# Inverse spectra of a long convolution: tiles of 128 rows, or slots of 32 rows

## The chip, the core and the metric

The kernel runs on one core of one Trainium2 chip. That core has five engines with queues of their own: PE (matrix products into PSUM), DVE (vector), ACT (activation and copies), POOL (general purpose) and SP (issues DMAs). The profile shows PE's weight loads as a sixth row, PEld. The metric is the device time of one execution in microseconds, lower being better. The kernel before has a median of 608.51 us in 3 runs (606.69 to 613.0).

## The reference

`u` has 2048 positions (L) and 640 channels (D). Two branches are mixed by a gate computed from the input.

```
dt = exp(log_dt);  A = -exp(log_A_real) + 1j * A_imag;  C = (C_real + 1j * C_imag) * dt
P  = exp((A * dt)[:, :, None] * pos)                       # 640 x 128 x 2048
K  = 2.0 * einsum("dn,dnl->dl", C, P).real                 # the filter of each channel
a  = irfft(rfft(u_t, 4096) * rfft(K, 4096), 4096)[:, :, :2048] + u * D_skip
b  = irfft2(rfft2(x) * (w_r + 1j * w_i))                   # over positions and channels
g  = sigmoid((x * gate_w).sum(-1));   out = g * a + (1 - g) * b
```

The change is in branch `a`, in the product of the two spectra and the transform back.

## The kernel before, in words

All transforms are matrix products in fp32. The 640 channels are worked in four column chunks `c` of 160. A transform of length 4096 is split in two stages. Stage one (`stage1`) turns blocks of the input into 33 partial spectra, one for each residue `k` of 0 to 32 (the others follow by symmetry), and ACT copies them into the tile `t1`. Stage two (`stage2`) multiplies the slice of one `k` by a 128x128 table (`w2`), as two matmuls with 64 output columns each: real and imaginary part of 64 frequencies. Two residues share the 128 PSUM lanes; such a pair is called a group here, and there are 16 groups and a half one (`k` = 32).

The program has these parts. `phase_a` computes the spectra of `u` and stores them in DRAM (`u_d`), then computes branch `b`, whose last tiles go to DRAM as `s3e_d`. `phase_b` computes the filters `K` beside it and stores them in `k_d`. `phase_c` begins with the filters' stage one for chunk 0. `phase_d` does the rest, and all edits that change instructions lie in it:

- `fronts` computes stage two of the filter for two groups at a time into one two-bank PSUM tile (`p_s`), and multiplies it by the spectrum of `u` (`us`, loaded from `u_d` on ACT's queue): `ma` (L798) holds the products re x re and im x im, `mb` (L799) the crossed ones. The difference (L803) and the sum (L804) go to `t2`, real parts on lanes 0 to 63 and imaginary on 64 to 127, each for one `k`. Since each output of 64 lanes comes from one half of `ma` or `mb`, there are four such instructions of 64 lanes for two groups, two on DVE and two on POOL.
- `backs` multiplies `t2` by the inverse table `w3`, one 128x128 table per `k`, as two matmuls of 64 columns (`p_i`, L817), ACT copies the PSUM tile to `s3`, and a DMA on ACT's queue stores it in `s3_d`.
- `load_c` loads `s3_d` again with the lanes exchanged (`t`, issued by SP), and `last_c` does the last inverse stage (`p_c`, L896), multiplies by the gate into `ot` and adds branch `b`. `load_e` and `last_e` do the like for branch `b` (`t3e` from `s3e_d`, `p_e`, L161, then `oe`, L879).
- `first` is the filter's stage one for the next chunk (`p_s`, L336).

A chunk has five steps: four of four groups and one of the half group. In each step `merge` interleaves three streams by due times: `mains` (fronts of this step, then backs of a step two earlier: `late` holds two), `last_e` or `last_c`, and `first`. The order on each engine is then settled by a scheduler that follows this program order and its own estimates of when operands are ready. Each engine works strictly in its own order.

PSUM has eight banks: in `phase_d` a pool `c_ps` of three tiles of two banks, shared by stage one, stage two and the inverse step, and a pool `d_ps` of two banks for `p_e` and `p_c`. A tile is taken in turn; its next user waits until the reader of the last one is done.

Of the kernel before, what the change touches and what calls it, by code (L numbers as in the profile page):

```python
# [49 lines left out]


def _tables():
# [14 lines left out]
    e3 = np.zeros((64, 2, 2, 32))  # L67
    for j in range(2):
        e3[:, j, j, :] = kr

    e3e = np.zeros((32, 4, 4, 32))
    for r in range(4):
# [3 lines left out]
        e1[0], e1[1], e3.reshape(4, 32, 64).swapaxes(0, 1).reshape(128, 64), e3e.reshape(128, 128), np.eye(128), one,  # L76
# [7 lines left out]
    c, s = np.cos(ph), np.sin(ph)  # L84
    w2 = np.concatenate([np.concatenate([c, -s], 2), np.concatenate([s, c], 2)], 1)
# [7 lines left out]
    w3 = np.swapaxes(w3, 0, 1).reshape(128, NP * 128)  # L93
# [37 lines left out]
    return {"t_c1": f(c1), "t_w2": f(w2), "t_w3": f(w3), "t_td": f(td),  # L131
# [3 lines left out]
def _lay_out(u, log_a, a_i, c_r, c_i, log_dt, d_skip, w_r, w_i, gate_w):  # L135

    ul = u.reshape(32, 64, 4, 40, 4).transpose(2, 4, 0, 3, 1)[:, JR][..., A_ORDER].reshape(4, 128, 40, 64)
    f = (np.arange(18).reshape(9, 2, 1) + 32 * np.arange(64)) % L
# [46 lines left out]
def body(tc, A, out):  # L185
    nc = tc.nc
    T = Ctx()
    with ExitStack() as top:
# [3 lines left out]
        T.s3_d = dram.tile([4, 64, 64, 160], F32, name="s3_d")  # L192
# [161 lines left out]
def phase_a(tc, A, T):  # L354
# [90 lines left out]
    with ExitStack() as ctx:  # L445
# [25 lines left out]
        def front(pr, st):  # L471
            nl = st.nl = 128 if pr < 8 else 64
            st.w3 = w3p.tile([128, 2, 128], F32, tag="w3", name="w3")
            nc.sync.dma_start(st.w3[:, 0:nl // 64, :], w3v[:, 16 + 2 * pr:16 + 2 * pr + nl // 64, :])
# [262 lines left out]
def phase_c(tc, A, T, ctx):  # L737
# [10 lines left out]
    T.w3 = T.cc.tile([128, NP, 128], F32, name="w3")  # L748
# [20 lines left out]
def phase_d(tc, A, T, ctx, out):  # L769
# [9 lines left out]
    ps = ctx.enter_context(tc.tile_pool(name="c_ps", reuse_waits="tile", bufs=3, space=PSUM))  # L779
    pd = ctx.enter_context(tc.tile_pool(name="d_ps", reuse_waits="tile", bufs=2, space=PSUM))  # L780

    def load(c, g0, gn, st):
        nl = st.nl = 128 if g0 < 16 else 64
        st.us = up.tile([128, 4, 2, 160], F32, tag="us", name="us")
        nc.scalar.dma_start(st.us[:nl, 0:gn], T.u_d[c, :nl, g0:g0 + gn])

    def fronts(c, g0, gn, st):
        nl, us = st.nl, st.us
        nj = nl // 64

        t2 = st.t2 = wk.tile([128, 8, 160], F32, tag="t2", name="t2")
        for h in range(0, gn, 2):
            hn = min(2, gn - h)
            pv, _ = stage2(nc, ps, T.w2, T.t1[c], g0 + h, hn)
            uu = us[:nl, h:h + hn]
            ma = wk.tile([128, 2, 2, 160], F32, tag="ma", name="ma")
            mb = wk.tile([128, 2, 2, 160], F32, tag="mb", name="mb")
            V.tensor_tensor(out=ma[:nl, :hn], in0=pv, in1=uu, op=ALU.mult)  # L798
            V.tensor_tensor(out=mb[:nl, :hn], in0=pv, in1=uu[:, :, ::-1, :], op=ALU.mult)  # L799
            for j in range(nj):  # L800
                l = slice(64 * j, 64 * j + 64)
                o = slice(nj * h + j, nj * (h + hn), nj)
                (G if j else V).tensor_tensor(out=t2[0:64, o, :], in0=ma[l, :hn, 0, :], in1=ma[l, :hn, 1, :], op=ALU.subtract)  # L803
                (V if j else G).tensor_tensor(out=t2[64:128, o, :], in0=mb[l, :hn, 0, :], in1=mb[l, :hn, 1, :], op=ALU.add)  # L804
            yield 0.55 * hn

    def backs(c, g0, gn, st):
        t2 = st.t2
        s3 = w2k.tile([128, 8 if gn > 1 else 1, 160], F32, tag="s3%d" % min(2, gn), name="s3")
        np_ = gn * st.nl // 64  # L810
        k0 = 2 * g0
        for h in range(0, np_, 4):
            hn = min(4, np_ - h)
            p = ps.tile([128, 2, 512], F32, tag="ps", name="p_i2")
            for i in range(hn):
                for x in (0, 64):
                    T.mm = P.matmul(p[x:x + 64, i // 2, 160 * (i % 2):160 * (i % 2) + 160], T.w3[:, k0 + h + i, x:x + 64], t2[:, h + i, :], start=True, stop=True)  # L817
# [102 lines left out]
    for c in range(4):  # L920
        if c < 3:
            fst = T.first(c + 1, ps)
        for g in range(5):
# [3 lines left out]
            if c and g == 1:  # L927
                load_c(c - 1, 0, 32)
# [52 lines left out]
```

## Time and profile before

| | |
|---|---|
| median of 3 runs | 608.51 us (606.69 to 613.0) |
| span of the profiled execution, first to last instruction | 605.9 us |
| mean granted PE clock | 0.963 |
| busy share of the span | PE 89%, DVE 82%, PEld 68%, ACT 60%, POOL 43% |
| DMA | 101.96 MB, mean 168 GB/s |
| first product `ma` of `phase_d` | at 437.7 us |

The three runs shown have no time of the profiled execution itself beside its span: the median lies 2.6 us above the span, which stands for what lies around it. A row of the timeline gives start, length, engine, line, operation, output and inputs, tile shape and count; a matmul's length includes its latency, so rows of PE overlap and their work is read from start to start. An fp32 matmul leaves two records. A row `[x <-Y]` says that the engine stood idle for x us until Y released it. In a row of the groups the number after the bar is the busy time, then the mean length in ns.

### The profile page before, as it was taken

The numbers are of one execution on the slowest core, as the hardware profiler recorded it, in microseconds if no ns is written. First come the engines' busy times: TensorE is split into PE (matmuls) and PEld (weight loads), VectorE is DVE, ScalarE is ACT, GpSimd is POOL, SyncE is SP. The second block draws the span as 40 slices with busy tenths as digits, with TensorE's granted clock in tenths as the row PEclk, the third lists the DMA queues.
The fourth block names the chain that finished last, engine by engine and source line by source line (L and its number), as shares of the span: only waits on it lengthen the run. The fifth ranks groups of instructions, "written<-read, shape, count | busy, mean of one in ns | idle before, by whom it ended". The sixth has DMA issues, their size and how long they took to land. (4 is left out here: it accounts for less than half of the span.)

```text
span 605.9 us, 16674 instructions
## 1 busy us (share of the span) xinstructions
PE 537.6 (89%) x7084; PEld 409.0 (68%) x7084; DVE 496.4 (82%) x748; ACT 364.5 (60%) x659; POOL 263.0 (43%) x246
## 2 busy tenths in 40 slices
PE   9598979988989989989889989898969999999875
PEld 7586647766766667666667676656859877787651
DVE  5971597598899998999998899879397696995965
ACT  4556775476857777899697897798712322232120
POOL 4931153054346344444515344416253447547533
PEclk9999999999979997999897999999998999999979
DMA  8777203235612321243250232006684989879767
GB/s 342 292 283 264 90 2 130 92 133 196 245 45 66 100 85 41 79 125 125 67 140 22 55 96 110 29 23 212 212 346 146 364 274 287 313 254 322 241 211 269
DMA packets 48082, 101.96 MB, mean 168 GB/s; under 512 B 3316, under 2 KB 32776, under 8 KB 46248
## 3 DMA queue, kind: packets, MB, share of 16 engines
q1 hardware_dynamic: 24888, 67.74, 32.1%
q10 hardware_dynamic: 20080, 22.52, 11.9%
q0 software_dynamic: 3040, 10.65, 5.3%
q8 instruction: 55, 0.90, 0.6%
q14 instruction: 19, 0.16, 0.1%
HBM read 60.91 MB, written 39.98 MB: 167 GB/s over the span
## 5 line engine op out<-in xcount | busy, mean ns | idle before, releaser
L349 PE MATMUL p_s<-t,w 128*64 128x160 f32 x1056 | 91.6, 311 | 11.2 <-ACT ut L383 6.0
L681 POOL TENSOR_TENSOR y<-e,sc 128x512 f32<-128x512 f32 x40 | 55.4, 1384 | 89.2 <-DVE x L676 46.7
L349 PEld LDWEIGHTS p_s<-t,w 128*64 128x64 f32 x1056 | 75.9, 137 | 22.3 <-ACT ut L383 6.6
L641 ACT ACTIVATE e<-p_e 128x512 f32<-128x512 f32 x120 | 68.6, 602 | 23.6 <-PE p_e L639 21.4
L683 POOL TENSOR_TENSOR y<-e,sc 128x512 f32<-128x512 f32 x40 | 55.5, 1388 | 44.9 <-ACT sc L667 32.0
L696 PE MATMUL p_k<-x,y 128*32 128x64 f32 x2560 | 63.0, 227 | 11.2 <-POOL y L681 6.1
L696 PEld LDWEIGHTS p_k<-x,y 128*32 128x32 f32 x2560 | 45.2, 112 | 39.6 <-issue 24.2
L552 PE MATMUL p_eo<-td,pmt 107*128 107x321 f32 x204 | 67.5, 450 | 3.9 <-ACT pmt L506 3.9
L337 ACT COPY t<-p_s 128x512 f32<-128x512 f32 x40 | 24.5, 621 | 69.0 <-PE p_s L336 45.5
L653 DVE SCALAR_TENSOR_TENSOR q<-q,p_p 128x512 f32<-128x512 f32 x80 | 53.4, 680 | 13.5 <-ACT q L652 13.3
L639 PE MATMUL p_e<-rm,par 128*128 128x512 f32 x120 | 58.9, 520 | 5.2 <-ACT e L641 3.7
L803 POOL TENSOR_TENSOR t<-ma 64x320 f32<-64x320 f32 x32 | 27.9, 873 | 64.2 <-DVE ma L798 54.8
L652 ACT ACTIVATE q<-p_p 128x512 f32<-128x512 f32 x80 | 46.4, 591 | 6.6 <-PE p_p L650 6.2
L552 PEld LDWEIGHTS p_eo<-td,pmt 107*128 107x128 f32 x204 | 37.7, 194 | 18.4 <-ACT pmt L506 6.4
L678 DVE TENSOR_TENSOR x<-e,cx 128x1024 f32<-128x1024 f32 x40 | 48.5, 1212 | 1.9 <-ACT cx L669 1.9
L817 PE MATMUL p_i<-t,w 128*64 128x160 f32 x528 | 45.1, 308 | 4.4 <-POOL t L804 3.4
L336 PE MATMUL p_s<-c,kt 128*64 128x128 f32 x640 | 44.3, 277 | 3.9 <-DVE mb L799 2.0
L336 PEld LDWEIGHTS p_s<-c,kt 128*64 128x64 f32 x640 | 39.5, 138 | 12.2 <-issue 6.9
L650 PE MATMUL p_p<-rp,par 128*128 128x512 f32 x80 | 43.3, 546 | 4.6 <-DVE q L653 4.5
L819 ACT COPY s<-p_i 128x640 f32<-128x640 f32 x32 | 21.8, 693 | 38.8 <-PE p_i L817 38.7
L817 PEld LDWEIGHTS p_i<-t,w 128*64 128x64 f32 x528 | 39.1, 141 | 8.9 <-POOL t L804 4.0
L798 DVE TENSOR_TENSOR ma<-p_s,us 128x640 f32<-128x640 f32 (+1 forms) x36 | 28.2, 784 | 20.3 <-PE p_s L349 13.3
(153 smaller groups left out, 1186.4 us busy)
## 6 DMA issues: line engine op xcount, KB each, us to landing
u_d<-ut SPq DMA_DIRECT2D x32, 320.0 KB, 3.2
us<-u_d ACTq DMA_DIRECT2D x16, 640.0 KB, 6.0
s_d<-s ACTq DMA_DIRECT2D x15, 640.0 KB, 6.7
t<-s_d SPq DMA_DIRECT2D x14, 640.0 KB, 5.7
ww<-in_w_l SPq DMA_DIRECT2D x8, 642.0 KB, 3.8
ue<-u_d SPq DMA_DIRECT2D x8, 640.0 KB, 4.1
k_d<-kt SPq DMA_DIRECT2D x4, 1280.0 KB, 8.7
kt<-k_d SPq DMA_DIRECT2D x8, 640.0 KB, 5.9
```

Of the source, the lines that this page charges most:

```text
L336: nc.tensor.matmul(p[64 * ri:64 * ri + 64, j, :], src(i + j), e1[ri], start=True, stop=True)
L349: ins = nc.tensor.matmul(p[64 * j:64 * j + 64, i, 160 * ri:160 * ri + 160], w2[:, x, 64 * ri:64 * ri + 64], t1[:, x // 2 if x < 32 else K0 ...
L552: P.matmul(p[:, :E], st.pmt[:DC, c, w, j, :], tv[:DC, w, c, :], start=c == 0, stop=c == 2)
L639: P.matmul(p[:, :], pars[t], rm[:, c:c + 512], start=True, stop=True)
L641: st.exp = S.activation(ef[:, c:c + 512], p[:, :], AF.Exp)
L652: S.activation(qf[:, c:c + 512], p[:, :], AF.Copy, bias=MAGIC)
L653: V.scalar_tensor_tensor(out=qf[:, c:c + 512], in0=qf[:, c:c + 512], scalar=MAGIC, in1=p[:, :], op0=ALU.subtract, op1=ALU.subtract)
L678: V.tensor_tensor(out=x[:, 0].rearrange("p d (h j) -> p d h j", h=2), in0=e[:, :, 0:64].rearrange("p d (h j) -> p d h j", h=2), in1=cx.uns ...
L681: ins = G.tensor_tensor(out=y[:, 1], in0=e[:, :, 64:96], in1=sc[:, 0], op=ALU.mult)
L683: G.tensor_tensor(out=y[:, 0], in0=e[:, :, 64:96], in1=sc[:, 1], op=ALU.mult)
L696: P.matmul(st.pb[32 * r:32 * r + 32, o, :], y[:, ri, 4 * qq + JR[r], :], x[:, ri, 4 * qq + JR[r], :], start=t % 2 + qq + 1 - ri == 0, stop ...
L817: T.mm = P.matmul(p[x:x + 64, i // 2, 160 * (i % 2):160 * (i % 2) + 160], T.w3[:, k0 + h + i, x:x + 64], t2[:, h + i, :], start=True, stop ...
```

## The change

The 64 frequencies of each `k` are put in another order (`M_ORDER`): the even ones, and the odd ones mirrored with their conjugates. Then half a tile, 32 rows, is a spectrum of its own: the 128 lanes of a group are four slots of 32 rows, each with its own residue modulo 128 (`SLOTS`), and real and imaginary part lie beside each other in the free dimension. So:

- Products stay within lanes. `fronts` takes one group at a time (a one-bank `p_s`), with two products of 128x320 each; for two groups one subtraction on DVE and one addition on POOL, both of 128 lanes.
- `backs` works on a unit of four groups: for each of two halves `j` and each of real and imaginary part, eight matmuls of 32 rows and 64 columns (L855 of the new kernel), each of which uses one quarter of the array's rows and one half of its columns, into four banks, one for each slot. The imaginary part is added to the real part in PSUM. The table shrinks from 33 x 128 to 17 x 128 columns.
- The special residues (0, 64 and 32) are in group 8 and group 16: in the third unit of each chunk one matmul has 64 rows, and the half group is a 32-row spectrum of its own.
- A chunk has four steps of one unit, with other due times. `p_e` begins with the first step of a chunk (the second of chunk 0), `p_c` with the third. All four loads of `s3_d` are issued in the steps before and at that.
- PSUM: `c_ps` has four tiles of one bank, for stage one, stage two, `p_e` and `p_c` together; `c_pi` has one tile of four banks for the inverse step.
- A unit is stored in one DMA, after two copies; before, the last unit was stored in halves.

```diff
+SLOTS = [[k for x in (2 * g, 2 * g + 1) for k in (POS_K[x], 64 - POS_K[x])] for g in range(16)] + [[32, 32]]
+GROUPS = ((0, 1, 2, 3), (4, 5, 6, 7), (8, 9, 10, 11, 16), (12, 13, 14, 15))
...
-    T.w3 = T.cc.tile([128, NP, 128], F32, name="w3")
+    T.w3 = T.cc.tile([128, 17, 2, 64], F32, name="w3")
...
-    ps = ctx.enter_context(tc.tile_pool(name="c_ps", reuse_waits="tile", bufs=3, space=PSUM))
-    pd = ctx.enter_context(tc.tile_pool(name="d_ps", reuse_waits="tile", bufs=2, space=PSUM))
+    ps = ctx.enter_context(tc.tile_pool(name="c_ps", reuse_waits="tile", bufs=4, space=PSUM))
+    pi = ctx.enter_context(tc.tile_pool(name="c_pi", reuse_waits="tile", bufs=1, space=PSUM))
...
+    def fronts(c, u, st):
+        t2 = st.t2 = wk.tile([128, 5, 2, 160], F32, tag="t2", name="t2")
+        gs = GROUPS[u]
+        for h in range(0, len(gs), 2):
+            hn = min(2, len(gs) - h)
+            l = slice(0, 128) if hn > 1 else slice(32, 64)
...
             for i in range(hn):
+                pv = spectra(c, gs[h + i])[l]
+                V.tensor_tensor(out=ma[l, i], in0=pv, in1=st.us[l, h + i], op=ALU.mult)
+                V.tensor_tensor(out=mb[l, i], in0=pv, in1=st.us[l, h + i, ::-1, :], op=ALU.mult)
+                yield 0.55
+            V.tensor_tensor(out=t2[l, h:h + hn, 0], in0=ma[l, :hn, 0], in1=ma[l, :hn, 1], op=ALU.subtract)
+            G.tensor_tensor(out=t2[l, h:h + hn, 1], in0=mb[l, :hn, 0], in1=mb[l, :hn, 1], op=ALU.add)
+
+    def backs(c, u, st):
+        t2, gs = st.t2, GROUPS[u]
+        s3 = w2k.tile([128, 4, 320], F32, tag="s3", name="s3")
+        p = pi.tile([128, 4, 512], F32, tag="pi", name="p_i2")
+        for j in range(2):
+            todo = []
+            for s in range(4):
+                for x in range(2):
+                    i, l = 2 * j + x, slice(32 * s, 32 * s + 32)
+                    if gs[i] == 8 and s < 2:
+                        i, l = (0, slice(0, 64)) if s == 0 else (4, l)
+                    todo.append((p[64 * x:64 * x + 64, s, 160 * j:160 * j + 160], l, i))
+            for ri in range(2):
+                for o, l, i in todo:
+                    T.mm = P.matmul(o, T.w3[l, gs[i], ri], t2[l, i, ri], start=ri == 0, stop=ri == 1)
+            yield 0.55
+        for s in (0, 2):
+            S.copy(s3[:, s:s + 2], p[:, s:s + 2, 0:320])
+        T.sd = nc.scalar.dma_start(T.s3_d[c, 32 * u:32 * u + 32].rearrange("(x k) a d -> (k a) x d", k=4), s3.rearrange("p s (j d) -> p (s j) d", j=2))
...
-            if g - (c == 0) in (1, 2):
-                beside = [last_e(c, AG * (g - 1 - (c == 0)))]
+            if g - (c == 0) in (0, 1):
+                beside = [last_e(c, AG * (g - (c == 0)))]
...
-            if c in (1, 2) and g > 2:
-                beside += [last_c(c - 1, AG * (g - 3))]
+            if c in (1, 2) and g > 1:
+                beside += [last_c(c - 1, AG * (g - 2))]
```

The order on PE at the start of `phase_d`, before: from behind the first stage two (`p_s_5595`, L349, two groups) to the first `p_e` (L161). L336 is stage one of the next chunk.

```order
L336 MATMUL p_s_5613<-c_65,kt 64x128 x8
L349 MATMUL p_s_5623<-t_5276,w_68 64x160 x8
L336 MATMUL p_s_5640<-c_65,kt 64x128 x8
L349 MATMUL p_s_5653<-t_5276,w_68 64x160 x8
L336 MATMUL p_s_5670<-c_65,kt 64x128 x8
L349 MATMUL p_s_5680<-t_5276,w_68 64x160 x8
L336 MATMUL p_s_5697<-c_65,kt 64x128 x8
L349 MATMUL p_s_5710<-t_5276,w_68 64x160 x8
L336 MATMUL p_s_5732<-c_65,kt 64x128 x8
L349 MATMUL p_s_5742<-t_5276,w_68 64x160 x8
L336 MATMUL p_s_5765<-c_65,kt 64x128
L161 MATMUL p_e<-t3e,c_65 64x480 x4
```

The same place after the change: stage two is L378 now, stage one L365, the inverse step L855 and `p_e` L190.

```order
L378 MATMUL p_s_5595<-t_5276,w_68 64x160 x4
L365 MATMUL p_s_5603<-c_65,kt 64x128 x8
L378 MATMUL p_s_5613<-t_5276,w_68 64x160 x4
L378 MATMUL p_s_5624<-t_5276,w_68 64x160 x4
L365 MATMUL p_s_5631<-c_65,kt 64x128 x8
L378 MATMUL p_s_5641<-t_5276,w_68 64x160 x4
L365 MATMUL p_s_5650<-c_65,kt 64x128 x8
L378 MATMUL p_s_5666<-t_5276,w_68 64x160 x4
L855 MATMUL p_i_5827<-t_5592,w_5268 64x160 x32
L190 MATMUL p_e<-t3e,c_65 64x480 x2
```

The first `p_e` has come nearer to the start: twelve groups of stage two and five tiles of stage one stood ahead of it, now five groups, three tiles and one unit of the inverse step.

In chunk 1, on PE, the first `p_c` (L896 before, L929 after) reads `t`, the loaded copy of all of chunk 0's `s3_d`. Before, the twelve rows up to that `p_c`; the last inverse matmuls of chunk 0 (`p_i_6101`) stand seven rows further up, with two stages two, one stage one and three `p_e` behind them:

```order
L336 MATMUL p_s_6170<-c_65,kt 64x128 x8
L817 MATMUL p_i_6181<-t_5953,w_5268 64x160 x8
L161 MATMUL p_e<-t3e,c_65 64x320 x2
L817 MATMUL p_i_6195<-t_5953,w_5268 64x160 x8
L349 MATMUL p_s_6209<-t_5612,w_68 64x160 x8
L336 MATMUL p_s_6232<-c_65,kt 64x128 x8
L349 MATMUL p_s_6242<-t_5612,w_68 64x160 x8
L336 MATMUL p_s_6264<-c_65,kt 64x128 x8
L817 MATMUL p_i_6275<-t_6036,w_5268 64x160 x8
L817 MATMUL p_i_6291<-t_6036,w_5268 64x160 x8
L349 MATMUL p_s_6307<-t_5612,w_68 64x160 x2
L896 MATMUL p_c<-t_6031,c_65 64x480 x4
```

And after, from the last unit of chunk 0 (`p_i_6156`) on:

```order
L855 MATMUL p_i_6156<-t_5867,w_5268 64x160 x16
L190 MATMUL p_e<-t3e,c_65 64x320 x2
L365 MATMUL p_s_6179<-c_65,kt 64x128 x8
L855 MATMUL p_i_6156<-t_5867,w_5268 64x160 x16
L378 MATMUL p_s_6215<-t_5602,w_68 64x160 x4
L855 MATMUL p_i_6296<-t_5965,w_5268 64x160 x32
L855 MATMUL p_i_6405<-t_6089,w_5268 64x160 x32
L929 MATMUL p_c<-t_6083,c_65 64x480 x2
L365 MATMUL p_s_6228<-c_65,kt 64x128 x8
```

Between the end of chunk 0's last unit and the first `p_c` there are now one group of stage two and two units of the inverse step; chunk 2 has the same rows. Stage one and two of the rest of the step stand behind that `p_c`.

136 lines of the change are left out of this document (66 added, 70 removed).

## The prediction

> **What bounds the kernel now.** The page comes first: no engine is idle enough to ignore. Then busy times by stretch, cut where the first product of each column chunk starts (`ma`, L798) and where the last inverse matmul ends.
>
> ```profile
> PE 537.6 (89%) x7084; PEld 409.0 (68%) x7084; DVE 496.4 (82%) x748; ACT 364.5 (60%) x659; POOL 263.0 (43%) x246
> ...
> 437.60:475.20 37.60, 32.22 (x418) 28.95 (x416) 29.54 (x41) 10.24 (x16) 15.47 (x17) 0.95 0.74 266
> 475.20:515.00 39.80, 37.48 (x478) 31.14 (x476) 33.17 (x48) 11.67 (x19) 22.65 (x25) 1.00 0.92 304
> 515.00:555.20 40.20, 37.67 (x474) 30.54 (x472) 33.19 (x48) 11.65 (x19) 22.23 (x25) 1.00 0.85 293
> 555.20:588.00 32.80, 26.44 (x308) 21.43 (x306) 29.29 (x41) 6.81 (x11) 16.88 (x19) 0.95 0.79 252
> 588.00:605.90 17.90, 11.76 (x52) 3.41 (x48) 9.06 (x23) 0.69 (x1) 5.84 (x5) 0.88 0.72 244
> ```
>
> The columns are stretch, length, busy PE, PEld, DVE, ACT and POOL, granted clock, DMA share, GB/s. In the four chunks PE and DVE are both near full: PE 37.5 of 39.8 us in the second, DVE 29.3 of 32.8 in the fourth. DMA stands at 0.74 to 0.92. The order of instructions on all engines is that of before up to about 430 us, so only these 168 us can change.
>
> PE's work is read from the timeline, start to start, since the records overlap.
>
> ```profile
> 515.58 1.31 PE L349 MATMUL p_s<-t,w 128*64 128x160 f32 x16
> 516.72 1.04 PE L336 MATMUL p_s<-c,kt 128*64 128x128 f32 x16
> 517.59 2.34 PE L817 MATMUL p_i<-t,w 128*64 128x160 f32 x32
> 519.83 1.36 PE L349 MATMUL p_s<-t,w 128*64 128x160 f32 x16
> 521.02 0.97 PE L161 MATMUL p_e<-t3e,c 128*64 128x480 f32 x4
> 521.83 0.93 PE L336 MATMUL p_s<-c,kt 128*64 128x128 f32 x14
> ```
>
> Two groups of stage two cost 1.14 us (0.57 a group), four of stage one 0.87, a unit of the inverse step (32 records) 2.24, that is 0.07 a record on two column tiles, a `p_e` of 480 columns 0.80 (0.54 for 320, in proportion). A middle chunk is then 17 x 0.57 + 10 x 0.87 + 4.3 (`p_e`) + 4.3 (`p_c`) + 132 x 0.07 = 36.2 us, 0.91 of its 39.8.
>
> **Products, DVE and POOL.**
>
> ```profile
> 440.98 0.82 DVE L798 TENSOR_TENSOR ma<-p_s,us 128x640 f32<-128x640 f32 x1
> 441.72 0.82 DVE L799 TENSOR_TENSOR mb<-p_s,us 128x640 f32<-128x640 f32 x1
> 442.45 0.64 DVE L803 TENSOR_TENSOR t<-ma 64x320 f32<-64x320 f32 x1
> 443.12 1.06 DVE L804 TENSOR_TENSOR t<-mb 64x320 f32<-64x320 f32 x1
> 444.22 0.82 DVE L798 TENSOR_TENSOR ma<-p_s,us 128x640 f32<-128x640 f32 x1
> ...
> 577.48 0.47 DVE L798 TENSOR_TENSOR ma<-p_s,us 64x320 f32<-64x320 f32 x1
> 577.87 0.47 DVE L799 TENSOR_TENSOR mb<-p_s,us 64x320 f32<-64x320 f32 x1
> ...
> L902 DVE TENSOR_TENSOR ot<-ot,oe 128x320 f32<-128x320 f32 x1 | 0.5, 493 | 0.0
> ```
>
> Two groups cost DVE 3.24 us (440.98 to 444.22). After, there are four products of 320 columns, 0.39 start to start, and one subtraction of 128x320. Its nearest row is the lone 128x320 sum, 0.49; the upper bound is L804's 1.06, which ran beside POOL. That makes 2.05 to 2.6; I take 2.1, by the sum's row, since POOL now starts one sum where it had two. Over 32 pairs DVE loses 36 us, POOL half of its 64x320 sums. The gain is not on the path one for one: DVE falls to some 25 us a chunk, and PE becomes the bound. DMA, 0.85 of 40.2 us or 34 a chunk with almost the same bytes, stays below PE.
>
> **The inverse step, PE.** Before, 264 matmuls give 528 records; after, 16 units of 32 matmuls give 1024. On eight tiles side by side a record costs a quarter of 0.07: 64 x 0.0175 = 1.12 us a unit. No row of before splits the array by rows; the nearest splits it by columns into four:
>
> ```profile
> 432.60 1.10 PE L696 MATMUL p_k<-x,y 128*32 128x64 f32 x64
> ...
> 131.39 0.30 PE L696 MATMUL p_k<-x,y 128*32 128x64 f32 x2
> 131.62 0.50 PE L650 MATMUL p_p<-rp,par 128*128 128x512 f32 x1
> 132.05 0.32 PE L696 MATMUL p_k<-x,y 128*32 128x64 f32 x8
> 132.30 0.79 PE L349 MATMUL p_s<-t,w 128*64 128x160 f32 x8
> 133.02 0.54 PE L696 MATMUL p_k<-x,y 128*32 128x64 f32 x24
> 133.49 0.79 PE L349 MATMUL p_s<-t,w 128*64 128x160 f32 x8
> ```
>
> 64 records of 64 columns start in about 0.9 us (1.10 less a record's tail), 14 ns each: 56 ns on its tile, so all four run together, and the queue delivers a start every 14 ns. The bounds: 1.12 us a unit if rows split as columns do, 4.5 if row tiles take turns and only the two column tiles run together. I take 1.12, by that row.
>
> TensorE: Matmul & The Clock Gate, a page of the Trainium skill, says under "Wait — 56ns, not 53.3ns?" that starts never come closer than about 25 ns. By it 1024 records would take an estimated 25.6 us, 7.7 more than the sum; the 14 ns row speaks against it.
>
> Each change of tile shape costs time: eight `p_s` records from 132.30 take 0.72 instead of 0.56, 24 `p_k` from 133.02 take 0.47 instead of 0.34. I take 0.14 a change. In the last 168 us there is none before (all is 128*64); after, by the order, the units stand in some 27 stretches (54 changes), four units hold 64-row matmuls among the others (16), and the 32-row spectrum adds 8. So the inverse step is 16 x 1.12 + 78 x 0.14 = 29 us, against 528 x 0.07 = 37. **PE gains only 8 us.**
>
> **Two waits that the order creates.** Stage one, stage two, `p_e` and `p_c` now take turns on PE with less between them and their loads.
>
> ```profile
> PE p_e L161 <- DMA t3e<-s3e_d: 2.7, 1, 2.7
> ...
> 436.29 1.36 PE L349 MATMUL p_s<-t,w 128*64 128x160 f32 x16 [0.51 <-ACT t L337]
> 437.89 0.32 SPq L857 DMA_DIRECT2D t3e<-s3e_d  x1
> 453.39 2.22 PE L161 MATMUL p_e<-t3e,c 128*64 128x480 f32 x8 [2.69 <-DMA t3e<-s3e_d]
> 437.00:450.00 13.00, 11.01 (x168) 10.21 (x166) 12.10 (x16) 2.94 (x5) 7.20 (x8) 1.00 0.97 395
> ```
>
> First: `t3e`, issued at 437.9, landed at 453.4 while DMA was full (0.97). After, 1.06 MB of `w3` less is loaded before it (2.7 us at 395 GB/s), but the third `us` load is issued earlier; I take 451. PE reaches that `p_e` after five groups, three of stage one and a unit (2.9 + 2.6 + 1.4 = 6.9 us), about 444.5 with DVE's and POOL's part. It stands there some 6.5 us; behind it wait stage one and two, and so ACT and DVE.
>
> Second: in chunks 1 and 2 the first `p_c` stands three items behind the last unit that it depends on.
>
> ```profile
> 480.51 1.29 ACT L819 COPY s<-p_i 128x640 f32<-128x640 f32 x2 [1.80 <-PE p_i L817]
> ...
> s_d<-s ACTq DMA_DIRECT2D x15, 640.0 KB, 6.7
> ...
> t<-s_d SPq DMA_DIRECT2D x14, 640.0 KB, 5.7
> ```
>
> Copies 1.4 with their releases, store 6.7, load 5.7: with issue 14.0 us from that unit's end. Before, the order keeps PE 15 us of work in between. After, there are one group (0.57) and two units, each behind the copies of the one before (one `p_i` buffer): 2 x (1.6 + 1.4) = 6.0. PE stands still 8 us, twice; DVE's `ot` heads its queue too, and nothing makes it up, since PE is the bound. Bounds: 3 us each if store and load take 2.6 and 3.7 as at the end (rows below), 10 if stores queue.
>
> **Tail.**
>
> ```profile
> 586.03 2.43 PE p_i L817 x16
> ...
> 588.48 0.70 ACT s L819
> ...
> 589.21 2.63 DMA s_d<-s
> ...
> 591.90 3.65 DMA t<-s_d
> ```
>
> Before, the last unit leaves in halves. After, one store follows two copies: +0.7, the larger store +1.0, matmuls -1.0. From the last group's matmuls to the span's end I take 24 us: 20.6 from the unit's start (19.9 before), 2.5 for its products, 0.7 for the copies of the unit before it.
>
> **Sum.** From 451 us PE has left 59 groups (33.6, +1.2 for the 32-row spectra), 27 of stage one (23.5), `p_e` 17.2, `p_c` 8.6, 14 units (25.4): 109.5 us. At 0.93 busy (0.91 now, less waiting for DVE) that is 117.7; with 2 x 8 the last group ends at 584.7, the span at 608.7, 2.8 above 605.9. The median of the runs lies 2.6 above the profiled span: **611 us.**
>
> **Rivals.** *The waits don't bite*: if `t` and `t3e` land before PE arrives, 16 us go: 595. For it: before, only 2.7 us were lost to `t3e`. Against: the distances in the order. *Row tiles take turns*: if the eight tiles run four at a time, a unit is 2.24 + changes, 14 x 1.12 / 0.93 = 17 us more: 628; two at a time, 51 more: 662. The point from which it decides is 25 ns a record (17.5 + 8 us / 1024), where PE's gain is gone; at that floor the 14 units cost 7 us more: 618. For it: no row shows row tiles; against: the column tiles and their 14 ns. It ends slower than before, and it is also the rival in which the change doesn't do what it says. TensorE: Matmul & The Clock Gate of the Trainium skill ("Measured speedup vs the span model") gives four row tiles 3.07 times, not four; by an estimate from it the units' 17.9 us would be 23.3 and the time 617, which no run here shows. *Four PSUM banks are too few*: 39 tiles a chunk share one ring where 28 and 12 had two; at 0.85 busy the sum is 11 more: 622.
>
> **How the numbers follow.** Forecast 0.42 (604 to 618); waits don't bite 0.22 (590 to 603); row tiles 0.22, of which 0.06 at the floor of 25 ns (616 to 620), 0.11 four at a time (622 to 632), 0.05 two; ring 0.14 (616 to 626). The range, 595 to 630, leaves a tenth on each side. One per cent, 6 us, is what a measurement tells from no change. Below 602.4: most of the second and a little of the first, 0.22; within: most of the forecast, 0.35; above 614.6: 0.43.
>
> **What would show it.** `ma` and `mb` at 0.47 us and DVE near 25 us a chunk; records of `p_i` 17 ns apart inside a unit (35 or 70: row tiles take turns); PE waiting on `t3e` once near 445 to 451 and on `t<-s_d` twice for about 8 us; the first 430 us as before. Wrong would be: no such waits, or PE well under 0.9 busy outside them.

## The result, and the profile after

The changed kernel takes **627.9 us** (median of 6 runs, 626.5 to 633.9) against 607.6 us of the kernel before (6 runs, 603.6 to 613.0). The ratio is 1.036, with a 95% interval of 1.029 to 1.042: slower by about 20 us. The forecast was 611, with a range of 595 to 630. The sign was the likeliest one and the time lies inside the range, but the central number missed by 17 us. The profile below is that of the longest of the six runs, 633.9 us.

First the page of the kernel after: busy time of the engines, and the products' group (line, operation, count, busy time, mean ns of one, idle time ahead of it and its releaser).

```profile
PE 540.1 (85%) x7580; PEld 396.9 (63%) x7580; DVE 463.1 (73%) x780; ACT 362.9 (57%) x655; POOL 235.8 (37%) x214
...
L835 DVE TENSOR_TENSOR ma<-p_s,us 128x320 f32<-128x320 f32 (+1 forms) x68 | 33.1, 487 | 35.8 <-PE p_s L378 35.6
```

DVE is relieved, from 496.4 to 463.1 us, by products of 0.49 us (0.47 was forecast). Yet a product now waits 35.6 us in all for stage two on PE. PE's total has hardly changed (537.6 before, 540.1 now), so its share says little. What it waited for, in the window from 430 us to the end, says more (total us, times, longest).

```profile
PE p_c L929 <- issue: 20.1, 2, 11.1
PE p_e L190 <- DMA t3e<-s3e_d: 8.0, 1, 8.0
PE p_i L855 <- ACT s L858: 6.7, 5, 2.4
PE p_c L929 <- DMA t<-s_d: 5.9, 1, 5.9
```

"Issue" at `p_c` is a load of `t3` for which the profile names no releaser; it comes up once in chunk 1 and once in chunk 2, 11.1 and 9.0 us. DVE and POOL, for which PE had stood here and there before (`oe`, `mb`, `t`), are gone from this list. No wait at stage one or two in it is above 0.5 us, so the ring of four PSUM banks isn't what PE waits for. Two rows of the same query on the kernel before, where `p_c` had hardly waited for its load:

```profile
PE p_e L161 <- DVE oe L879: 3.5, 4, 0.9
...
PE p_c L896 <- DMA t<-s_d: 1.0, 1, 1.0
```

The same stretch as a table by column chunk, cut where the first `ma` of each chunk starts and where the last `ma` of all starts. The columns are stretch, length, busy PE, PEld, DVE, ACT and POOL, granted clock, DMA share, GB/s.

```profile
440.94:478.35 37.41, 29.44 (x446) 23.58 (x442) 21.32 (x50) 7.66 (x13) 8.71 (x9) 0.86 0.71 257
478.35:531.06 52.71, 39.47 (x606) 28.38 (x604) 24.65 (x55) 12.46 (x20) 14.61 (x16) 0.87 0.66 216
531.06:582.27 51.21, 39.82 (x598) 29.07 (x596) 24.70 (x57) 11.33 (x18) 16.32 (x18) 0.83 0.66 219
582.27:604.05 21.78, 21.78 (x414) 14.81 (x410) 19.34 (x47) 5.15 (x8) 9.38 (x11) 1.00 0.87 295
604.05:631.95 27.90, 14.71 (x160) 6.73 (x158) 10.98 (x27) 2.57 (x4) 6.78 (x7) 0.80 0.77 262
```

Chunks 1 and 2 took 39.8 and 40.2 us before and take 52.7 and 51.2 now; that is more than the whole loss. The last chunk, in which PE never waits, is full (PE 21.78 of 21.78) and shorter than before. DVE needs 24.7 us in a middle chunk where it needed 33.2: the forecast said about 25.

One such wait in PE's timeline (start, length, count of records, in brackets the idle time ahead).

```profile
495.39 0.80 PE L855 MATMUL p_i<-t,w 32*64 32x160 f32 x32
496.12 0.79 PE L378 MATMUL p_s<-t,w 128*64 128x160 f32 x8
497.64 1.37 PE L855 MATMUL p_i<-t,w 32*64 32x160 f32 x64 [0.73 <-ACT s L858]
500.43 1.37 PE L855 MATMUL p_i<-t,w 32*64 32x160 f32 x64 [1.42 <-ACT s L858]
512.89 1.87 PE L929 MATMUL p_c<-t,c 128*64 128x480 f32 x4 [11.10 <-issue]
514.51 1.95 PE L365 MATMUL p_s<-c,kt 128*64 128x128 f32 x16
516.22 2.38 PE L378 MATMUL p_s<-t,w 128*64 128x160 f32 x16
518.36 1.06 PE L929 MATMUL p_c<-t,c 128*64 128x480 f32 x4
```

The unit that ends at 496.2 is the last of chunk 0. Behind it stand one group and two units, as the prediction counted, and then the first `p_c` of chunk 1, which PE reaches at 501.8 and starts at 512.9. The three rows behind it are slow: 1.87 us for a `p_c` that takes 0.97 elsewhere, 1.95 and 2.38 for rows of 1.04 and 1.31. The granted clock, third from the end of each row, shows why.

```profile
503.00:504.00 1.00, 0.00 (x0) 0.00 (x0) 0.00 (x0) 0.00 (x0) 0.00 (x0) 1.00 1.00 300
504.00:505.00 1.00, 0.00 (x0) 0.00 (x0) 0.00 (x0) 0.00 (x0) 0.00 (x0) 0.93 0.84 270
505.00:506.00 1.00, 0.00 (x0) 0.00 (x0) 0.00 (x0) 0.00 (x0) 0.00 (x0) 0.50 1.10 355
...
513.00:515.00 2.00, 2.00 (x10) 0.94 (x12) 0.14 (x1) 0.00 (x0) 0.00 (x0) 0.50 0.36 112
515.00:517.00 2.00, 2.00 (x20) 1.99 (x18) 0.52 (x1) 0.50 (x1) 1.20 (x1) 0.50 0.00 0
517.00:519.00 2.00, 2.00 (x16) 1.72 (x15) 1.43 (x4) 0.11 (x1) 0.38 (x1) 0.62 0.00 0
```

The clock falls to half some 3 us after PE's last matmul, and rises again only in the last row, at 518.5 by finer rows, 5.6 us after PE has started: a wait of 11 us costs more than 11 us. The same happens behind `t3e`.

```profile
445.67 1.36 PE L855 MATMUL p_i<-t,w 32*64 32x160 f32 x64
455.01 1.86 PE L190 MATMUL p_e<-t3e,c 128*64 128x480 f32 x4 [7.97 <-DMA t3e<-s3e_d]
```

### The profile page after: what moved, and what is told of

It reads as the page before. It is cut to its first block, busy times and chain, and to the rows that moved or that the text cites. A ratio compares the mean times of both kernels' runs of the same rounds, so it can differ in the third digit from the quotient of the medians.

```text
span 631.9 us, 17674 instructions
## 1 busy us (share of the span) xinstructions
PE 540.1 (85%) x7580; PEld 396.9 (63%) x7580; DVE 463.1 (73%) x780; ACT 362.9 (57%) x655; POOL 235.8 (37%) x214
## 4 chain that ended last, share of the span: by engine, by line
PE 53%; DVE 20%; DMA 14%; issue 5%; ACT 5%; POOL 2%; DVEq 0%; SPq 0%; ACTq 0%; POOLq 0%
PE p_s L365 9%; PE p_s L378 9%; PE p_eo L581 7%; PE p_e L668 5%; DMA t3e<-s3e_d 4%; PE p_k L725 4%; DMA s_d<-s 4%; DMA u_d<-ut 4%; DVE q L682 3%; PE p_e L190 3%; PE p_i L855 3%; PE p_t L532 3%; PE p_p L679 2%; PE p_c L929 2%; PE p_i L595 2%
## 5 line engine op out<-in xcount | busy, mean ns | idle before, releaser
L378 PE MATMUL p_s<-t,w 128*64 128x160 f32 x1040 | 97.3, 324 | 10.6 <-ACT ut L412 7.5
L378 PEld LDWEIGHTS p_s<-t,w 128*64 128x64 f32 x1040 | 77.1, 144 | 24.3 <-ACT ut L412 8.4
L725 PE MATMUL p_k<-x,y 128*32 128x64 f32 x2560 | 63.4, 227 | 11.1 <-POOL y L710 6.1
L839 POOL TENSOR_TENSOR t<-mb 128x320 f32<-128x320 f32 (+1 forms) x36 | 34.6, 962 | 79.0 <-DVE mb L836 65.1
L835 DVE TENSOR_TENSOR ma<-p_s,us 128x320 f32<-128x320 f32 (+1 forms) x68 | 33.1, 487 | 35.8 <-PE p_s L378 35.6
L365 PEld LDWEIGHTS p_s<-c,kt 128*64 128x64 f32 x640 | 39.5, 144 | 14.0 <-issue 11.2
L929 PE MATMUL p_c<-t,c 128*64 128x480 f32 (+1 forms) x96 | 23.9, 615 | 25.9 <-issue 20.1
L365 PE MATMUL p_s<-c,u 128*64 128x128 f32 x640 | 43.1, 285 | 2.5 <-ACT ut L412 2.5
L365 PE MATMUL p_s<-c,kt 128*64 128x128 f32 x640 | 43.9, 285 | 0.9 <-ACT q L681 0.7
```

The source lines that it names most:

```text
L365: nc.tensor.matmul(p[64 * ri:64 * ri + 64, j, :], src(i + j), e1[ri], start=True, stop=True)
L378: ins = nc.tensor.matmul(p[64 * j:64 * j + 64, i, 160 * ri:160 * ri + 160], w2[:, x, 64 * ri:64 * ri + 64], t1[:, x // 2 if x < 32 else K0 ...
L725: P.matmul(st.pb[32 * r:32 * r + 32, o, :], y[:, ri, 4 * qq + JR[r], :], x[:, ri, 4 * qq + JR[r], :], start=t % 2 + qq + 1 - ri == 0, stop ...
```

## The experiments

Theory A: the loss is made by waits that PE stands in order, `p_c` behind the store and load of a chunk's last unit and `p_e` behind `t3e`, with the slow clock behind each. The rivals: the new inverse step itself is dear; or DMA is full, and what is regained here is lost there. Times carry the noise of the first 430 us, in which the order is that of before (in the profiles the first `ma` starts anywhere between 433.7 and 444.8 us), so beside them stands the length from the first `ma` to the span's end, called the last part: 168.2 us before, 191.0 after.

**One dependency taken away.**

```diff
             src = T.s3_d[c, 32 * y:32 * y + 32].rearrange("k (x a) d -> k x a d", x=2)
+            if c < 2 and y == 3:
+                src = T.u_d[c, 96:128, 0:16].rearrange("k g r d -> k (g r) d").rearrange("k (x a) d -> k x a d", x=2)
```

> The changed kernel, except that in chunks 1 and 2 the fourth quarter of `t3` (the rows that the last unit of the chunk before stores) is loaded from another DRAM table of the same size, which is ready from the start; every store, load, matmul and copy stays, only the dependency of that load on the last unit's store goes, so the output isn't the reference's. Theory A (the first `p_c` stands 11 us each behind store and load, and PE runs slowly for some 3 us after it): chunks 1 and 2 fall from 52.7 and 51.2 us to about 38 to 40 each, the time to 628 - 26 = 602 us (597 to 606). Rival 1 (the loss is the inverse step's own work, twice as many records and the changes of tile shape, and the wait is only where it shows): 622 us or more, PE waits elsewhere for as long. Rival 2 (store and load are slow because DMA is full, and the next reader is late too): about half is regained, 615 us.

Measured: 605.6 us, ratio to before 1.000 (0.996 to 1.004); last part 173.0 us, chunks 1 and 2 at 41.1 and 43.9, in a profile of the longest of its eleven runs (616.6 us). So as much as the whole loss, 22 us, hangs on this one load of chunks 1 and 2, and rival 1 is out as the main cause. PE still waits 2.8 and 5.1 us at `p_c`. The third quarter of `t3`, whose load is issued only at 493.8, is the likely reason; the profile doesn't show when it landed.

**Both waits taken away.**

```diff
 src = T.s3_d[c, 32 * y:32 * y + 32].rearrange("k (x a) d -> k x a d", x=2)
+if c < 2:
+    src = T.u_d[c, 32 * y:32 * y + 32, 0:16].rearrange("k g r d -> k (g r) d").rearrange("k (x a) d -> k x a d", x=2)
...
-halved(nc, p[:, 0:n], T.e3e, t3es[c][:, a + i:a + i + n])
+x = T.t1[0].rearrange("p x d y -> p (x d y)")[:, 0:2560].rearrange("p (a d) -> p a d", a=16) if c == 0 else t3es[c]
+halved(nc, p[:, 0:n], T.e3e, x[:, a + i:a + i + n])
```

> The changed kernel with both kinds of wait taken away: all of `t3` of chunks 0 and 1 is loaded from a DRAM table of the same size that is ready from the start, and `p_e` of chunk 0 reads a tile of stage one that is in SBUF, in place of `t3e`; stores, loads and matmuls are as many as before, the output isn't the reference's. Theory A: nothing is left of the loss but the tail and the changes of tile shape; 596 us (591 to 601), the time that the rival in which the waits don't bite gives. If the inverse step's own work were dearer than on the old form: 608 or more.

Measured: 588.4 us, ratio 0.972 (0.965 to 0.978), 8 us less than expected and below the expected range. The table by chunk of this kernel, columns as above:

```profile
437.90:464.10 26.20, 26.20 (x446) 21.79 (x442) 21.32 (x50) 7.67 (x13) 8.79 (x9) 1.00 1.00 385
464.10:499.51 35.41, 35.41 (x598) 25.65 (x596) 25.13 (x56) 11.89 (x20) 15.64 (x16) 1.00 0.87 291
499.51:536.26 36.75, 36.02 (x598) 25.69 (x596) 25.27 (x56) 10.68 (x18) 16.34 (x18) 1.00 0.86 303
536.26:558.96 22.70, 22.70 (x422) 15.20 (x418) 19.53 (x46) 6.43 (x10) 8.29 (x10) 1.00 0.94 301
558.96:586.20 27.24, 15.28 (x160) 6.77 (x158) 11.11 (x27) 2.57 (x4) 6.78 (x7) 0.80 0.81 263
```

PE is busy without a gap, at full clock, in three of the four chunks: it is the bound, as the prediction said it would become. Set beside the table of the kernel after, this prices the waits: chunk 0 costs 37.4 - 26.2 = 11.2 us more, chunk 1 52.7 - 35.4 = 17.3, chunk 2 51.2 - 36.8 = 14.5. The two last rows hardly differ. Of the 42.7 us in all, 33.1 are idle time of PE (length less busy: 45.8 against 12.7) and 9.6 are longer busy time (145.2 against 135.6) for the same matmuls: the slow clock.

**The distance restored by the order, `p_c` later.**

```diff
-            if c in (1, 2) and g > 1:
-                beside += [last_c(c - 1, AG * (g - 2))]
+            if c in (1, 2) and g == 3:
+                beside += [last_c(c - 1, 0), last_c(c - 1, AG)]
```

> The changed kernel with both halves of `last_c` in chunks 1 and 2 in step 3, where they stand in steps 2 and 3: one step of PE's work (about 9 us) more between the last unit and the first `p_c`; the computation is whole. Theory A: the wait of 11 us falls to 0 to 3, twice, the time is 603 us (598 to 609). Rival 1 (the work itself): 622 or more. Rival 2 (DMA full): 612 to 618, since store and load then end as late as before but PE has other work for only a part.

Measured: 617.0 us, ratio 1.018 (1.012 to 1.024); last part 177.7. PE's waits:

```profile
PE p_c L929 <- DMA t<-s_d: 12.8, 2, 6.9
...
PE p_c L929 <- issue: 6.0, 1, 6.0
```

The waits fell from 11.1 and 9.0 to 6.9 and 6.0 us, not to 0 to 3 (the other 5.9 of the first row is that of the span's end, which the kernel after has too). The step bought 3 to 4 us, not 9. The time is that of rival 2, but the timeline shows another reason: the edit made less distance than expected.

```profile
498.46 1.96 PE L855 MATMUL p_i<-t,w 32*64 32x160 f32 x64 [1.34 <-ACT s L858]
```

In this profile the last unit of chunk 0 ends at 490.2, and this row, the last ahead of `p_c`, at 500.4. That is 10.2 us of PE's way where the kernel after has 5.6, so 4.6 us more, and the wait is 4.2 us shorter; store and load took 10.5 and 4.9 us, as in the kernel after. So distance counts about one for one, and a step is worth half of what was expected. Whether store and load are slow because of other transfers is asked by the next run.

**The store's competitor held back.**

```diff
             if g == 3 and c < 3:
-                load_e(c + 1)
+                with behind(T.ld):
+                    load_e(c + 1)
```

> The changed kernel, except that the loads of `t3e` for chunks 2 and 3 (1.28 MB each) are issued behind the last quarter of `t3`, where they are issued just ahead of the store on which that quarter depends; the computation is whole. Theory A, second part (store and load take 14 to 16 us instead of the 12.4 that I took because 1.28 MB of `t3e` and 0.64 MB of `kt` move at the same time): the store falls from 10.3 and 9.4 us to about 6, PE's wait from 11.1 to 6 or 7, twice, the time is 617 us (613 to 621). Rival (the store is slow by its own pattern of 640-byte pieces, and DMA has room): the store stays above 9 us, the time at 625 to 630.

Measured: 621.3 us, ratio 1.026 (1.018 to 1.034); last part 179.9. First a row of the kernel after on its transfers between 496 and 509 us (the last number is the median us to landing, of the store in question and the one behind it), then two pieces of the chain of waits of this kernel (start, length, what):

```profile
s_d<-s ACTq DMA_DIRECT2D x2, 640.0 KB, 9.9
```

```profile
490.30 6.89 DMA s_d<-s
...
497.21 4.22 DMA t<-s_d
```

The store takes 6.9 us without `t3e` beside it, which is what the prediction had taken (6.7), and PE's longest wait for `t3` falls from 11.1 to 7.0, as theory A's second part said. In chunk 2 the store takes 4.6 us (9.4 in the kernel after). The stores that now come just behind `t3e`, issued at 498.6 and 544.1, take 9.3 and 9.4. The time stands between both expectations and just above theory A's range, so the time alone doesn't decide; the stores' durations do.

**Units one step earlier.**

```diff
-        while len(late) > (1 if i > 12 else 2):
+        while len(late) > 1:
```

> The changed kernel with one number changed: a block's inverse unit runs at the end of the next step throughout, where it runs two steps later up to the last steps; so the last unit of a chunk is stored a step before its readers' step. The computation is whole. Theory A: some 9 us of PE work stand between that unit and the first `p_c`; the wait falls from 11 to about 4 us, twice, the slow matmuls after it mostly go: 608 us (603 to 614). Rival (the work itself, and the waits only move): 620 or more, with PE waiting for `t2` of POOL instead.

Measured: 607.5 us, ratio 1.002 (0.998 to 1.007); last part 169.7.

```profile
PE p_c L929 <- DMA t<-s_d: 9.0, 2, 8.2
...
PE p_c L929 <- issue: 4.0, 1, 4.0
```

One number of the order takes away the whole loss. The wait in chunk 1 is 4.0 us as expected, in chunk 2 it is 0.9 (the 8.2 is at the span's end), and no wait for `t2` of POOL takes its place. The computation, the number of tiles and the bytes are those of the changed kernel: what made it slow is where the unit stands. The edit does two things at once: PE's way between unit and `p_c` grows from 5.6 to 10.8 us (483.9 to 494.7), and the store now ends before `t3e` is issued (load at 492.1, `t3e` at 493.2), so that it takes at most 6.8 us (485.3 to 492.1).

**`p_e` later in chunk 0.**

```diff
-            if g - (c == 0) in (0, 1):
-                beside = [last_e(c, AG * (g - (c == 0)))]
+            if c and g < 2:
+                beside = [last_e(c, AG * g)]
+            elif not c and g == 2:
+                beside = [last_e(0, 0), last_e(0, AG)]
```

> The changed kernel with both halves of `last_e` of chunk 0 in step 2, where they stand in steps 1 and 2; the computation is whole. Theory A: the stall of 8.0 us on `t3e` and the slow matmuls after it (about 2.5 us) go, the time is 618 us (615 to 621), the waits at `p_c` stay. Rival 1: 626 to 630, what PE gains there it loses to DVE, which then has all of `oe` in one step.

Measured: 627.3 us, ratio 1.037 (1.029 to 1.045): nothing gained. PE still waits 6.0 us for `t3e` and 1.5 us for that of chunk 1; the last part is 187.2 us, 4 less than after, which the time doesn't show. The time is the one that rival 1 gave (626 to 630). Theory A's expectation fell here, as far as the profile shows, because the edit moved little: PE reaches `p_e` at 454.9 us instead of 447.0 in a profile whose `t3e` is issued 3.9 us later too, and the transfer took 16 us. A step of chunk 0 in which no `p_e` stands is short.

**The first `p_c` earlier in the kernel of before.**

```diff
-            if c in (1, 2) and g > 2:
-                beside += [last_c(c - 1, AG * (g - 3))]
+            if c in (1, 2) and g in (2, 3):
+                beside += [last_c(c - 1, AG * (g - 2))]
```

> The kernel of before with one edit: `last_c` of chunks 1 and 2 in steps 2 and 3 of five, where it stands in steps 3 and 4, so that the first `p_c` comes in the step that issues its load, as in the changed kernel; the inverse step is that of before. Theory A (distance alone makes the loss): PE stands some 8 us at each of the two, with 2 to 3 us of slow matmuls behind, the time is 608 + 2 x 10 = 628 us (622 to 636). Rival 1 (the new inverse step makes the loss): 606 to 612.

Measured: 609.6 us, ratio 1.004 (1.000 to 1.009), which is rival 1's time. But the edit didn't make the distance as short as it was meant to be, as PE's timeline shows:

```profile
480.26 2.35 PE L817 MATMUL p_i<-t,w 128*64 128x160 f32 x32
...
488.19 0.45 PE L817 MATMUL p_i<-t,w 128*64 128x160 f32 x4
...
506.36 0.62 PE L896 MATMUL p_c<-t,c 128*64 128x480 f32 x1
```

In this form of the kernel of before the last full unit of chunk 0 leaves PE at 482.6; behind it comes only the seventeenth group, 4 records that end at 488.6. The first `p_c` stands 18 us behind even that. The changed kernel has this group inside its third unit, so the last one stored is a full unit and ends 5.6 us of PE's way ahead of `p_c`. So the run is no test of theory A; it shows where the old order had its slack.

**PE kept busy during the wait.**

```diff
+            if c < 2 and a + i == 0:
+                fill = ps.tile([128, 512], F32, tag="ps", name="p_fill")
+                rhs = T.t1[c + 1].rearrange("p x d y -> p (x d y)")[:, 0:480]
+                with behind(T.mm):
+                    for x in range(28):
+                        P.matmul(fill[64 * (x % 2):64 * (x % 2) + 64, 0:480], T.e3, rhs, start=True, stop=True)
             p = ps.tile([128, 3, 160], F32, tag="ps", name="p_c")
```

> The changed kernel with work added: in front of the first `p_c` of chunks 1 and 2 stand 28 matmuls of 480 columns whose result is used nowhere, about 11 us at the pace of `p_e`, so that PE is busy while it waits for `t3`; the computation is whole. Theory (the matmuls after a wait run slowly because PE has stood still, as the granted clock of 0.61 behind the wait says): the first matmuls behind the wait run at 1.0, `p_c` 0.97 instead of 1.87 us, and 2.8 us are saved each time: 622 us (618 to 626), although PE does 22 us more. Rival (they are slow because DVE or the operands hold them up): they stay at 1.9 us, the time is 628 or more.

Measured: 633.0 us, ratio 1.041 (1.035 to 1.048); last part 192.8. PE's timeline, then the granted clock in rows of 1 us:

```profile
493.84 11.44 PE L931 MATMUL p_fill<-t,c 128*64 128x480 f32 x56
505.21 1.31 PE L855 MATMUL p_i<-t,w 32*64 32x160 f32 x54
508.55 1.75 PE L935 MATMUL p_c<-t,c 128*64 128x480 f32 x4 [2.03 <-DMA t<-s_d]
510.02 1.98 PE L365 MATMUL p_s<-c,kt 128*64 128x128 f32 x16
```

```profile
507.00:508.00 1.00, 0.00 (x0) 0.00 (x0) 0.00 (x0) 0.00 (x0) 0.00 (x0) 1.00 0.13 49
508.00:509.00 1.00, 0.45 (x2) 0.23 (x4) 0.00 (x0) 0.00 (x0) 0.00 (x0) 0.85 0.00 0
509.00:510.00 1.00, 1.00 (x4) 0.30 (x2) 0.00 (x0) 0.00 (x0) 0.00 (x0) 0.50 0.00 0
...
512.00:513.00 1.00, 1.00 (x17) 1.00 (x15) 0.27 (x1) 0.63 (x1) 0.35 (x1) 0.94 0.00 0
```

The 22.9 us more of matmuls cost little (a last part 1.8 us longer, 5 us by the medians of runs whose ranges overlap), which confirms that PE had stood idle there. But the gain didn't come, and the time is the rival's: a rest of 2.03 us of waiting was left (2.95 in chunk 2), and that was enough for the clock to fall to 0.50 for 3.4 us. So the test of the cause of the slow matmuls is inconclusive as an experiment; that they run at a granted clock of one half is read from the rows.

**A version with the waits gone and the computation whole.**

```diff
-        while len(late) > (1 if i > 12 else 2):
+        while len(late) > 1:
-            if c in (1, 2) and g > 1:
-                beside += [last_c(c - 1, AG * (g - 2))]
+            if c in (1, 2) and g == 3:
+                beside += [last_c(c - 1, 0), last_c(c - 1, AG)]
-    w2k = ctx.enter_context(tc.tile_pool(name="c_w2", reuse_waits="tile", bufs=2))
+    w2k = ctx.enter_context(tc.tile_pool(name="c_w2", reuse_waits="tile", bufs=3))
-        t3es[c] = dk.tile([128, 16, 160], F32, tag="t3e", name="t3e")
+        t3es[c] = T.te.tile([128, 16, 160], F32, tag="t3e", name="t3e")
+    T.te = pool("c_te", 1)
```

> The changed kernel with four edits that keep the computation whole: units one step after their block throughout, both halves of `last_c` of chunks 1 and 2 in step 3, three `s3` buffers instead of two, and `t3e` in a pool of its own in memory that is free earlier, so that its first load is issued ahead of `w3`'s. Theory A: no wait at `p_c`, that at `p_e` halved or gone, the tail 2 us shorter: 594 us (590 to 600), faster than both kernels. Rival (DMA, at 0.85 busy before, is the bound once PE doesn't wait): 603 to 608.

Measured: **590.1 us**, ratio to before 0.973 (0.966 to 0.980), last part 149.2, at the lower end of what was expected: faster than both kernels, and within 2 us of the kernel from which the waits were taken by force. Its longest wait:

```profile
PE p_c L930 <- DMA t<-s_d: 8.1, 1, 8.1
```

It is at the span's end; none of the others is above 1.4 us. DMA stands at 0.94 to 0.97 in chunks 1 and 2 without becoming the bound.

**The same without the early `t3e`.** The edit is the one before without its last three lines.

> The version that took 590.1 us (units one step after their block, late `last_c`, three `s3` buffers), without the pool of its own for `t3e`, so that its first load is issued behind `w3`'s and the store of `k_d` as in the changed kernel; the computation is whole. Theory A: the wait for `t3e` is worth its 8 us of idle and 3 us of slow matmuls by itself: 601 us (597 to 605), all of it in chunk 0. Rival (chunk 0 is bound by DMA or DVE, and PE catches up): 588 to 594.

Measured: 595.2 us, ratio 0.981 (0.972 to 0.990); last part 156.2, chunk 0 38.3 against 28.9 us. PE waits 7.4 us for `t3e`, and `p_e` takes 1.87 us behind it instead of 0.97. The wait is there in full, but by time it is worth about 5 us, by the last part 7.0: less than its 7.4 of idle and 3 of slow clock, so a part comes back later (chunks 1 and 2 are 0.7 and 0.9 us shorter, and the end 0.8). The time lies between the two expectations, and the intervals of the two versions overlap.

**The end.**

```diff
-    w2k = ctx.enter_context(tc.tile_pool(name="c_w2", reuse_waits="tile", bufs=2))
+    w2k = ctx.enter_context(tc.tile_pool(name="c_w2", reuse_waits="tile", bufs=3))
         for s in (0, 2):
             S.copy(s3[:, s:s + 2], p[:, s:s + 2, 0:320])
+            if s or (c, u) == (3, 3):
+                n, s = (2, s) if (c, u) == (3, 3) else (4, 0)
+                T.sd = nc.scalar.dma_start(T.s3_d[c, 32 * u + 8 * s:32 * u + 8 * (s + n)].rearrange("(x k) a d -> (k a) x d", k=4), s3[:, s:s + n].rearrange("p s (j d) -> p (s j) d", j=2))
...
+            for h in range(0, 32, 32 // parts):
+                for a in range(0, 16, w):
+                    T.ld = eng.dma_start(t3s[c][y + 4 * h:4 * h + 128 // parts:4, :, a:a + w], src[h:h + 32 // parts, :, a:a + w])
```

> The changed kernel with two edits at its end, the computation whole: three `s3` buffers instead of two, and the last unit stored and loaded in two halves of 16 rows, each behind its own copy, as before the change. Theory (the end of 29 us against 25 before comes of the copy that waits 4.1 us for an `s3` buffer, and of the one store of 5.7 us behind two copies): from the last `ma` to the span's end 24 us instead of 27.9, the time 624 us (620 to 627). Rival (the end is set by the chunk-2 matmuls and the slow clock there): 27 us as before, the time within 1 us.

Measured: 631.8 us, ratio 1.040 (1.034 to 1.046); from the last `ma` to the end 29.1 us. The theory fell, and the rival's time within 1 us wasn't met either:

```profile
601.75 1.37 PE L855 MATMUL p_i<-t,w 32*64 32x160 f32 x64 [1.42 <-ACT s L858]
...
616.09 7.43 PE L932 MATMUL p_c<-t,c 128*64 128x480 f32 x24 [8.52 <-DMA t<-s_d]
```

The last unit no longer waits for a buffer, and PE then waits 8.5 us instead of 5.9 for the last `t3`.

**The same edit on the version of 590.1 us.**

> The version with units one step after their block, late `last_c`, early `t3e` and three `s3` buffers (590.1 us in the run before), with the last unit in two halves as well; the computation is whole. Theory: the wait of 8.1 us for the last `t3` falls to 5, the time to 587 us (583 to 591). Rival (the halves' own stores take as long): 590.

Measured: 591.4 us (585.1 to 595.4), ratio 0.970 (0.965 to 0.976); the end 26.8 us against 28.4. That can't be told from 590.1, the rival's time. Why the end is 4 to 6 us longer in every kernel with the new units (22.7 before) stays open; a missing `s3` buffer and one large store are not the reason by themselves.

## Why the prediction was right and wrong

1. **Products on DVE and POOL: right.** 0.49 us each against 0.47, 24.7 to 25.3 us a middle chunk against about 25, and PE as the bound: busy in every microsecond of chunks 0, 1 and 3 once the waits are gone.

2. **Inverse step on PE: right.** 32 records took 0.80 us and 64 took 1.37, so a record costs 0.57 / 32 = 17.8 ns against the 17.5 forecast: eight tiles run side by side. A half of 32 records stands 0.73 us in the order (493.10 to 493.83), 0.16 more than 32 x 17.8 ns, and eight `p_s` ahead of it 0.67 instead of 0.57; that is 0.13 for each change of tile shape, and 0.14 was taken. The rival in which row tiles take turns is out, and so is a floor of 25 ns between starts.

```profile
492.43 0.74 PE L378 MATMUL p_s<-t,w 128*64 128x160 f32 x8
493.10 0.80 PE L855 MATMUL p_i<-t,w 32*64 32x160 f32 x32
493.83 0.76 PE L190 MATMUL p_e<-t3e,c 128*64 128x320 f32 x4
```

By the Trainium skill (TensorE: Matmul & The Clock Gate, "Measured speedup vs the span model") four row tiles give 3.07 times the pace, measured there at 512 columns. Here, at 160 columns, they give 3.8 times: 68 ns a record on 128 rows ((2.35 - 0.45) / 28, from the rows of the kernel of before with the early `p_c`) against 17.8.

3. **First wait: place right, size short.** PE reached `p_e` at 447.0 instead of 444.5 and `t3e` landed at 455.0 instead of 451: 8.0 us idle, 6.5 forecast. (In this profile the part from the first `ma` on starts 3.2 us later than in that of before, 440.9 against 437.7; counted from there PE came 0.7 us earlier and `t3e` landed 0.8 us later than forecast.) Chunk 0 lost 11.2 us against the kernel without waits.

4. **Second wait: mechanism and place right, size too small; this is the term that was off.** It was priced at 8 us each; PE stood 11.1 and 9.0, and with all that hangs on it chunks 1 and 2 lost 17.3 and 14.5, about twice the price. Its terms in chunk 1: copies 1.4 as taken; the store, issued at 497.6, was followed by its load at 508.0, so 10.4 instead of 6.7; the load 4.9 instead of 5.7; PE's work between 5.6 instead of 6.0. That makes 11.1 us. Two shorter waits of units for copies, 0.7 and 1.4, come on top; the prediction had them in its work. The mis-sized term is the store: 6.7 was the median of stores spread over the whole phase, while this one runs beside a `t3e` of 1.28 MB that the order starts 3 us earlier, and with `t3e` held back it took 6.9. The trace of before had stores of up to 9.7 us among those of this phase. The bound of 10 "if stores queue" was too low for chunk 1.

5. **A term that the sum hadn't: the slow clock.** 9.6 us of longer matmuls in all: 3.2, 4.1 and 3.8 in chunks 0, 1 and 2 (busy PE of the two tables), less 1.5 in the last two rows. In chunk 2 the clock had fallen before the long wait, in the short one of 1.42 us between the two units (row below, in the section on the hardware). The prediction read the granted clock in its table and didn't ask what a wait does to it; the kernel of before had shown it in small (`p_e` 2.22 us for 8 records behind 2.7 us of waiting, where two of 0.97 start 0.80 apart, at 0.95 clock in that chunk).

6. **The sum.** Its waits were 6.5 + 8 + 8 = 22.5 us, so without them it stood at 588.5; the kernel without waits took 588.4. That it fits to 0.1 us is luck, since three errors cancel. In the kernel without waits PE's work between the first `p_e` (442.7) and the last two units (557.8) is 113.7 us where the sum had 109.5: `p_e` 18.3 for 17.2, `p_c` 9.4 for 8.6, stage two with the 32-row spectra 38.3 for 34.8, the units 24.2 for 25.4, stage one as summed. Against that, PE works without a gap and not at 0.93, which is worth 8 us; so the last products start at 559.0, 3 us before the forecast's end of the last group less its waits (584.7 - 22.5 = 562.2). And the end takes 27.2 us, 3 more than the 24 of the forecast. With the waits at 11.2 + 17.3 + 14.5 = 43.0 in the profile, 39.5 by the medians (627.9 - 588.4), the miss of 17 us is that of the waits.

7. **Rivals.** "The waits don't bite" was priced at 595 because it left the 6.5 us of `t3e` in; without both waits it is 588. The ring of four banks shows no wait of PE. The rivals on slower's side ended near the measured time, one at 628, by mechanisms that didn't happen.

## What to carry to other kernels

A wait that a new order creates is the time from the last producer's end to the reader, copies, store and load with whatever shares the DMA just then, less the work that really stands between; the store's price is that of its busiest moment, not its median over a phase. When PE stands, add the matmuls behind the wait at half pace, for 3 to 6 us here: three waits of 8 to 11 us, 28 us in all, cost 43 us with the short waits and the slow clock around them. And when a change merges small pieces of work, look whether a small piece had been the last one and had hidden a round trip; here one number of the order (units one step after their block instead of two) was worth the whole loss, and with four small edits the change won 2.7%.

## What the runs showed of the hardware

The granted clock falls to exactly one half when PE stands still, 3.1 us after its last matmul in one case (501.8 to about 504.9), and after a gap of only 2.03 us in another; it came back 3.6 us after PE had started again in the kernel with the filling, and 5.5 to 5.6 us after it in the kernel after. A gap of 1.42 us can be enough. In chunk 2 of the kernel after, the clock is at 0.50 from 552.6 on, and the unit behind such a gap takes 2.44 us instead of 1.37:

```profile
552.68 2.44 PE L855 MATMUL p_i<-t,w 32*64 32x160 f32 x64 [1.42 <-ACT s L858]
```

The equal gap ahead of 500.43 in chunk 1 did nothing (the unit took 1.37 us). The stretches at half clock last 10.2, 13.7 and 17.1 us in chunks 0, 1 and 2 of the kernel after, 3.4 and 6.8 behind the filling, and 3.4 behind `t3e` in the kernel of before. All of these are whole multiples of 3.41 us, as if the clock were set anew once in 3.41 us and the place of a gap on that grid decided; no run tests that.

The Trainium skill (TensorE: Matmul & The Clock Gate, Part 1 on the clock gate) has the half rate after an idle window of about 3.4 us and the full rate after as long a busy one. The step of 3.41 us agrees; the gaps of 2.03 and 1.42 us are shorter than that, and the measurement decides: a gap of 1.4 us can be enough.

A 640 KB store took 10.4 us with a load of 1.28 MB beside it and 6.9 without that load, at the same size and pattern (9.4 and 4.6 in the next chunk). Row tiles of 32 rows gave 3.8 times the pace of 128 rows, at 17.8 ns a record of 160 columns on eight tiles.
